# Third contraction chunk of the expert layer as concurrent pairs of 64-row matmuls

## The chip, the cores and the metric

The kernel runs on one core of a Trainium2 chip. The metric is the device time of one execution in microseconds. Before the change it is 226.39 us, the median of three runs (226.37 to 228.31). The profiled execution has a span of 228.9 us, at a mean granted TensorE clock of 0.948.

## What is computed

A gated recurrence (an mLSTM cell) over 4 batches x 8 heads x 768 steps with head dimension 40 gives 3,072 tokens of 320 values. Each token then goes through one of eight experts, the one with the largest router logit:

```python
logits = x @ w_gate                              # [3072, 320] @ [320, 8]
expert_idx = np.argmax(logits, axis=1)
gate_w = softmax(logits)[np.arange(N), expert_idx]
for e in range(E):                               # rows of expert e
    h = np.maximum(x_sorted[lo:hi] @ w1[e], 0.0) # w1[e]: [320, 1024]
    y_sorted[lo:hi] = h @ w2[e]                  # w2[e]: [1024, 320]
y = gate_w[:, None] * y_sorted[inv_perm]
```

The change concerns `x_sorted @ w1[e]`. Its contraction is over 320 = 128 + 128 + 64, three chunks.

## The kernel before, in words

The first half (line 580, `for s in range(-3, NT)`) goes through the recurrence in 24 blocks of 128 tokens, all heads at once: scores, causal mask, attention-like products, a carried state, then router logits and the slot of every token in a DRAM buffer sorted by expert. All of it is recorded in an order written out by hand (`tc.manual_schedule()`, line 279): each engine takes its instructions in the order of the program text.

The second half is the expert layers. Work is cut into groups of `n` blocks of 128 tokens of one expert. Each expert has a first group with n = 2 (256 tokens) and a second with n = 1; six extra groups with n = 1 (`XU`) take what is over, their expert is known only at run time, and their weights are copied from the resident ones by `fetch` (line 758). A loop over further extras (line 812) is entered only if more are needed. The first groups of experts 0 and 1 ("early groups") are written into the end of the first half, in memory and PSUM buffers that the first half no longer needs; their output rows `zo` lie in the old `v1` buffers. The other groups follow in `order` (line 774), in the loop of line 788.

One group goes through these steps:

- `targets` or `aim`, then `turn` (line 226): TensorE transposes the tokens' rows, n x 3 transposes of 128 columns into one PSUM tile `tp`; VectorE copies it to `xT`. The third transpose takes columns 192 to 319 (`wch`), so that its upper 64 rows hold the third chunk and its lower 64 rows repeat columns of the second.
- `layer1` (line 236), in units `u` of 4/n feature blocks of 128: a unit is one PSUM bank `hp` of 512 columns. For every feature block three matmuls of 128 rows accumulate the chunks. The relu out of PSUM into `h` is VectorE's for even units and ScalarE's for odd ones. There are four units for n = 2, two for n = 1.
- `layer2` (line 255) per 128 tokens: eight matmuls of 320 columns accumulate in `zp`, in the order of the feature blocks; ScalarE copies to `zo`, and GpSimd starts a DMA that scatters the rows to `out`.

The transposes of the next group stand between layer 1 and layer 2 of the present one (`ready(groups[i + 1])`, line 799). Since TensorE's order is the program's, a wait at layer 2 holds the next group's layer 1.

The weights of all experts stay in SBUF as bf16: `w1_all` (line 160) has three chunks of 1,024 columns for each expert, in chunk three only rows 64 to 127 with data. Rows 0 to 63 of it are set to zero by VectorE (line 594, once in each of the iterations s = 0 to 7), so that a matmul over 128 rows adds nothing from them. `weights_in` and `weights_out` (lines 173 and 183) load one expert by three DMAs from GpSimd's software queue, converting from float32. They are called at points in the program text for expert after expert; the scatters of tokens and output rows share this queue. PSUM in the second half: three `hp` banks, three `zp`, two `tp` (line 733).

Of the kernel before, what the change touches and what calls it, by code (L numbers as in the profile page):

```python
# [8 lines left out]
F32 = mybir.dt.float32  # L9
BF16 = mybir.dt.bfloat16  # L10
# [5 lines left out]
PSUM = bass.MemoryType.PSUM  # L16
# [3 lines left out]
def kernel(  # L20
# [24 lines left out]
    DP = 64  # L45
# [11 lines left out]

    wch = [d0 if dsz == 128 else Dm - 128 for d0, dsz in dch]
    assert NT * 128 == N and FB * 128 == F and D <= DP
# [100 lines left out]
    w1_all = big.tile([128, DB, E, F], BF16)  # L160
# [12 lines left out]
    def weights_in(e0, n, dbs=((0, 2), (2, 3))):  # L173
        e = slice(e0, e0 + n)
        for a, b in dbs:
            d0, d1 = dch[a][0], sum(dch[b - 1])
            r = min(128, d1 - d0)
            nc.gpsimd.dma_start(
                w1_all[128 - r :, a:b, e, :].rearrange("p a e f -> p (a e) f"),
                moe_w1[e, d0:d1, :].rearrange("e (a p) f -> p (a e) f", p=r),  # L180
            )
# [44 lines left out]
    def turn(g):  # L226
        n = g["n"]
        src = g["xg"] if "xg" in g else xg[g["e"]][g["k"]]
        g["xT"] = spot("xT", [128, DB, n * 128], BF16)
        tp = spot("tp", [128, DB, n * 128], BF16)  # L230
        for j in range(n):
            for db in range(DB):
                nc.tensor.transpose(tp[:, db, j * 128 : (j + 1) * 128], src[:, j, wch[db] : wch[db] + 128], ident_b[:])
        nc.vector.tensor_copy(g["xT"], tp)

    def layer1(g, u):
        n = g["n"]
        per = 4 // n
        if u == 0:
            g["h"] = spot("h", [128, FB, n * 128], BF16)  # L240
        hp = spot("hp", [128, per, n * 128], F32)
        for i in range(per):
            fb = u * per + i
            for db in range(DB):
                nc.tensor.matmul(  # L245
                    hp[:, i, :], lhsT=g["w"][0][:, db, fb * 128 : (fb + 1) * 128], rhs=g["xT"][:, db, :],
                    start=(i == 0 and db == 0), stop=(db == DB - 1), skip_group_check=True,
                )
        dst = g["h"][:, u * per : (u + 1) * per, :]
        if u % 2 == 0:  # L250
            nc.vector.tensor_relu(dst, hp)  # L251
        else:
            nc.scalar.activation(dst, hp, AF.Relu)  # L253

    def layer2(g, j):
        zp = spot("zp", [128, Dm], F32)
# [23 lines left out]
    with tc.tile_pool(name="ring", bufs=1) as ring_pool, \  # L280
# [299 lines left out]
        for s in range(-3, NT):  # L580
# [12 lines left out]
            if 0 <= s < E:  # L593
                nc.vector.memset(w1_all[:64, DB - 1, s, :], 0.0)
# [48 lines left out]
        early = [dict(e=e, n=NE, k=0, si=0) for e in range(2)]  # L643
        spots.update(
            hp=[("sA", ps1), ("sB", ps1)], zp=[("tk", ps1), ("tq", ps1)], tp=[("dC", ps1)],
# [4 lines left out]
        for g in early:  # L650
            g["w"] = (w1_all[:, :, g["e"], :], w2_all[:, g["e"]])
# [43 lines left out]
    def extras():  # L695
# [37 lines left out]
        k: ctx.enter_context(tc.tile_pool(name="moe_" + k, bufs=n, space=PSUM)) for k, n in (("hp", 3), ("zp", 3), ("tp", 2))  # L733
# [24 lines left out]
    def fetch(ex):  # L758
        wx1 = wk_pool.tile([128, DB, F], BF16, name="wx1", bufs=XW)
        wx2 = wk_pool.tile([128, FB, Dm], BF16, name="wx2", bufs=XW)  # L760
        nc.sync.dma_start(wx1[:], w1_all[:, :, bass.ds(ex, 1), :].rearrange("p a e b -> p a (e b)"))
        nc.sync.dma_start(wx2[:].rearrange("p a b -> p (a b)"), w2_all[:, bass.ds(ex, 1)].rearrange("p e a b -> p (e a b)"))
        return wx1, wx2
# [8 lines left out]
    for e in range(E):  # L772
# [3 lines left out]
        dict(e=e, n=(NE, NJ - NE)[k], k=k, si=(0, NE)[k], w=(w1_all[:, :, e, :], w2_all[:, e])) for e, k in order  # L776
# [75 lines left out]
```

## Time and profile before

| | |
|---|---|
| time, median of 3 | 226.39 us |
| span of the profiled execution | 228.9 us |
| TensorE busy (matmuls) | 198.4 us, 87% |
| TensorE weight loads, beside matmuls | 167.9 us, 73% |
| VectorE / ScalarE / GpSimd busy | 56% / 52% / 56% |
| moved by DMA | 46.5 MB, mean 203 GB/s |
| layer 1 matmuls (line 245) in the stretch after 160 us | 312 of 128 columns, 96 of 256 columns |

A line of the timeline has the start in us, the time in us (from the start of the first to the end of the last of equal instructions in a row), the engine, the line in the kernel, the operation, `out<-in`, the shapes and the number of instructions; in brackets the idle time of the engine before it, and what ended it. "PE" is TensorE's matmuls, "PEld" its weight loads, "DVE" VectorE, "ACT" ScalarE, "POOL" GpSimd. Matmuls are pipelined, so the start of one to the start of the next is much less than the time of one; the ends are modelled. In the page's slices each digit is the busy share of 1/40 of the span in tenths, 9 being 90% or more.

### The profile page before, as it was taken

What the parts mean: (1) busy time and instruction counts of PE and PEld (TensorE: products, weight loads), DVE (VectorE), ACT (ScalarE), POOL (GpSimd) and SP (SyncE); (2) the same over time, 40 slices, a digit from 0 to 9 for tenths busy, and PEclk for the clock granted to TensorE, in tenths of its full rate; (3) what the DMA queues carried; (4) which work ended last, traced back from release to release, by engine and by line L of the source; (5) the groups of instructions that cost most, each with busy time, mean ns of one, the idle gap of its engine ahead of it and who ended that gap; (6) DMA issues with size and microseconds to landing.
All of it is one profiled execution on the core that took longest, in us unless ns stands there. A gap on an engine that the chain in (4) does not pass through costs nothing.

```text
span 228.9 us, 5771 instructions
## 1 busy us (share of the span) xinstructions
PE 198.4 (87%) x2054; PEld 167.9 (73%) x2063; DVE 128.4 (56%) x421; ACT 118.2 (52%) x275; POOL 129.2 (56%) x219
## 2 busy tenths in 40 slices
PE   2299999999999998899999968983999798989990
PEld 2168788889989998688788756862887586867760
DVE  7648778797678785877635423315454152333330
ACT  3458758789688887859321632430243333333330
POOL 5046696465678887679687298365455333333331
PEclk9999999999999999999855999997699999999996
DMA  7999999999999989999999999999999969966900
GB/s 138 178 190 190 188 203 168 203 207 207 171 164 188 167 161 175 201 162 169 163 314 194 190 149 176 252 224 218 220 265 212 239 247 369 386 231 248 366 28 4
DMA packets 122158, 46.50 MB, mean 203 GB/s; under 512 B 102474, under 2 KB 114893, under 8 KB 122128
## 3 DMA queue, kind: packets, MB, share of 16 engines
q1 hardware_dynamic: 107424, 27.52, 56.4%
q0 software_dynamic: 14240, 18.38, 38.7%
q8 instruction: 17, 0.28, 0.5%
q10 hardware_dynamic: 464, 0.21, 0.4%
q14 instruction: 13, 0.11, 0.2%
HBM read 39.38 MB, written 9.53 MB: 214 GB/s over the span
## 4 chain that ended last, share of the span: by engine, by line
PE 35%; DMA 26%; issue 16%; POOL 9%; DVE 8%; ACT 3%; POOLq 1%; SPq 0%; ACTq 0%
DMA w_all<-in_moe_w_dram 15%; POOL out_dram L265 8%; PE hp L447 7%; PE hp L379 6%; DMA out_dram<-zo,s_idx 6%; PE dC L387 4%; DMA v<-in_v_dram 4%; PE tk L341 3%; PE xt L424 3%; PE tq L341 3%; PE sA L354 2%; PE sA L359 2%; DMA kq<-in_q_dram 2%; PE hp L399 2%; DVE kq L88 1%
## 5 line engine op out<-in xcount | busy, mean ns | idle before, releaser
L265 POOL DMA_INDIRECT out_dram<-zo,s_idx x20 | 20.0, 998 | 31.2 <-ACT zo L263 22.7
L245 PEld LDWEIGHTS <-w_all 128*128 128x128 bf16 x384 | 31.4, 102 | 6.8 <-issue 2.5
L251 DVE TENSOR_SCALAR h<-hp 128x512 bf16<-128x512 f32 x26 | 18.0, 691 | 32.7 <-PE hp L245 30.8
L258 PE MATMUL zp<-w_all,h 128*128 128x320 bf16 x160 | 26.1, 310 | 8.2 <-DVE s_idx L207 4.9
L258 PEld LDWEIGHTS <-h 128*128 128x128 bf16 x208 | 18.4, 100 | 19.4 <-DVE h L251 6.9
L253 ACT ACTIVATE h<-hp 128x512 bf16<-128x512 f32 x26 | 15.5, 597 | 30.2 <-PE hp L245 20.3
L552 POOL DMA_INDIRECT x_sorted<-x_all,slots x24 | 25.0, 1043 | 10.6 <-ACT x_all L546 6.5
L245 PE MATMUL hp<-xT,w_all 128*128 128x128 bf16 (+1 forms) x336 | 30.0, 249 | 0.8 <-DMA w_all<-in_moe_w_dram 0.8
L417 POOL TENSOR_TENSOR x_sb<-x_sb,den 128x320 f32<-128x320 f32 x23 | 16.7, 725 | 21.0 <-DVE den L415 19.8
L263 ACT COPY zo<-zp 128x320 f32<-128x320 f32 x26 | 11.1, 425 | 25.6 <-PE zp L258 25.0
L379 PE MATMUL hp<-C_sb,qT 104*128 104x82 f32 x160 | 22.4, 286 | 0.5 <-DVE lgs L457 0.5
L379 PEld LDWEIGHTS hp<-C_sb,qT 104*128 104x128 f32 x160 | 21.1, 205 | 0.7 <-DVE lgs L457 0.6
L426 ACT COPY xT<-xt 128x384 f32<-128x384 f32 x24 | 11.6, 483 | 18.2 <-PE xt L424 13.3
L366 ACT CAST dB<-sB 128x512 bf16<-128x512 f32 x24 | 14.0, 582 | 12.6 <-PE sB L360 9.6
L341 PE MATMUL tk<-ident,kq 128*104 128x128 f32 x96 | 16.4, 296 | 4.0 <-DMA kq<-in_k_dram 4.0
L447 PE MATMUL hp<-wg_sb,xT 128*128 128x8 f32 x144 | 19.0, 264 | 0.0
L387 PE MATMUL dC<-vA,kq 128*104 128x82 f32 x160 | 18.6, 261 | 0.0
L447 PEld LDWEIGHTS hp<-wg_sb,xT 128*128 128x128 f32 x144 | 18.2, 203 | 0.0
L329 POOL CAST vAb<-vA 128x328 bf16<-128x328 f32 x24 | 11.0, 460 | 11.9 <-DVE vA L327 11.9
L367 POOL TENSOR_SCALAR_AFFINE_SELECT dB<-dB 128x512 bf16<-128x512 bf16 x24 | 16.3, 680 | 1.9 <-ACT dB L366 1.7
L327 DVE TENSOR_TENSOR vA<-v,G_T 128x328 f32<-128x328 f32 x24 | 15.3, 639 | 3.3 <-DMA v<-in_v_dram 3.2
L364 DVE TENSOR_TENSOR dA<-sA,cmask 128x512 bf16<-128x512 f32 x24 | 16.0, 665 | 1.9 <-PE sA L359 1.9
(150 smaller groups left out, 441.3 us busy)
## 6 DMA issues: line engine op xcount, KB each, us to landing
w_all<-in_moe_w_dram POOLq DMA_DIRECT2D x8, 640.0 KB
wx<-w_all SPq DMA_DIRECT2D x6, 768.0 KB
w_all<-in_moe_w_dram POOLq DMA_DIRECT2D x8, 512.0 KB
kq<-in_k_dram SPq DMA_DIRECT2D x24, 160.0 KB
kq<-in_q_dram SPq DMA_DIRECT2D x24, 160.0 KB
v<-in_v_dram SPq DMA_DIRECT2D x24, 160.0 KB
o_sb<-in_o_gate_dram SPq DMA_DIRECT2D x24, 160.0 KB
wx<-w_all SPq DMA_DIRECT2D x6, 640.0 KB
```

Of the source, the lines that this page charges most:

```text
L245: nc.tensor.matmul(hp[:, i, :], lhsT=g["w"][0][:, db, fb * 128 : (fb + 1) * 128], rhs=g["xT"][:, db, :], start=(i == 0 and db == 0), stop= ...
L251: nc.vector.tensor_relu(dst, hp)
L258: nc.tensor.matmul(zp, lhsT=g["h"][:, fb, j * 128 : (j + 1) * 128], rhs=g["w"][1][:, fb, :], start=(fb == 0), stop=(fb == FB - 1),)
L265: ins = nc.gpsimd.indirect_dma_start(out=out[:, :], out_offset=bass.IndirectOffsetOnAxis(ap=at, axis=0), in_=zo, in_offset=None, bounds_ch ...
L341: nc.tensor.transpose(tp[:, j, :], two(d[n], j), ident[:])
L364: nc.vector.tensor_tensor(d["dA"][:], sA[:], cmask[:, None, :].to_broadcast([128, PR, 128]), op=ALU.mult)
L367: nc.gpsimd.affine_select(d["dB"][:], d["dB"][:], compare_op=ALU.is_ge, fill=0.0, base=0, pattern=[[0, PR], [1, 128]], channel_multiplier=-1,)
L379: nc.tensor.matmul(hp[:, 2 * j * D1 : (2 * j + 2) * D1], lhsT=d["qT"][:, j, :], rhs=st["C"][:, j].rearrange("p h d -> p (h d)"), start=(j ...
L387: nc.tensor.matmul(st["dC"][:, j], lhsT=two(d["k"], j), rhs=d["vA"][:, 2 * j : 2 * j + 2, :], start=(c == 0 and j == 0), stop=True, skip_g ...
L417: eng.tensor_tensor(x3d, x3d, den[:].unsqueeze(2).to_broadcast([128, H, D]), op=ALU.mult)
L447: nc.tensor.matmul(lg[:, i * E : (i + 1) * E], lhsT=st[t]["xT"][:, db * 128 : (db + 1) * 128], rhs=wg_sb[:, db, :], start=(fresh and i == ...
L552: ins = nc.gpsimd.indirect_dma_start(out=xs[:, :], out_offset=bass.IndirectOffsetOnAxis(ap=slots[:, t : t + 1], axis=0), in_=x_all[:, t, : ...
```

## The change

The third chunk fills only half of the array's rows. The change runs it as pairs of matmuls over 64 rows each: the third chunk's weights of feature blocks 0 to 3 lie in partitions 0 to 63 and those of blocks 4 to 7 in partitions 64 to 127 ("folded"), and one matmul of each half runs in the lower and the upper 64 rows of the array at once, into two PSUM banks. The aim is to spend the time of half as many matmuls on the third chunk, and to drop the zeros.

What follows from it:

- the tokens' third chunk must lie in both halves of the partitions, so its transpose is made twice, each of 64 columns, into rows 0 to 63 and rows 64 to 127 of `tp`;
- units go in twos: at an even unit two `hp` banks are taken and the pairs for both written first; then the unit's two full chunks follow, and the odd unit's after it. Even units are feature blocks 0 to 3 (VectorE's relu), odd ones 4 to 7 (ScalarE's);
- `w1_all` has 2,560 columns for each expert instead of 3,072; the third chunk is loaded by two DMAs (one for each half) in place of one; the zeroing on VectorE is gone;
- PSUM has four `hp` and two `zp` banks. In the early groups `hp` goes through four banks (`sA`, `sB`, `tk`, `tq`), which `zp` shares.

```diff
-    w1_all = big.tile([128, DB, E, F], BF16)
+    w1_all = big.tile([128, E, FL * F + F // 2], BF16)
...
-    def weights_in(e0, n, dbs=((0, 2), (2, 3))):
-        e = slice(e0, e0 + n)
-        for a, b in dbs:
-            d0, d1 = dch[a][0], sum(dch[b - 1])
-            r = min(128, d1 - d0)
+    def weights_in(e, n=1):
+        nc.gpsimd.dma_start(
+            w1_all[:, e, : FL * F].rearrange("p (a f) -> p a f", f=F),
+            moe_w1[e, : FL * 128, :].rearrange("(a p) f -> p a f", p=128),
+        )
+        for i in range(2):
             nc.gpsimd.dma_start(
-                w1_all[128 - r :, a:b, e, :].rearrange("p a e f -> p (a e) f"),
-                moe_w1[e, d0:d1, :].rearrange("e (a p) f -> p (a e) f", p=r),
+                w1_all[64 * i : 64 * i + 64, e, FL * F :], moe_w1[e, FL * 128 :, i * HF * 128 : (i + 1) * HF * 128],
             )
...
-                nc.tensor.transpose(tp[:, db, j * 128 : (j + 1) * 128], src[:, j, wch[db] : wch[db] + 128], ident_b[:])
+                at = src[:, j, db * 128 : min(Dm, (db + 1) * 128)]
+                if db < FL:
+                    nc.tensor.transpose(tp[:, db, j * 128 : (j + 1) * 128], at, ident_b[:])
+                    continue
+                for r in range(2):
+                    nc.tensor.transpose(tp[64 * r : 64 * r + 64, db, j * 128 : (j + 1) * 128], at, ident_b[:])
...
-        hp = spot("hp", [128, per, n * 128], F32)
+        if u % 2 == 0:
+            g["hp"] = [spot("hp", [128, per, n * 128], F32) for _ in range(2)]
+            for i in range(per):
+                for a in range(2):
+                    c = FL * F + (v + i) * 128
+                    r = slice(64 * a, 64 * a + 64)
+                    nc.tensor.matmul(
+                        g["hp"][a][:, i, :], lhsT=w[r, c : c + 128], rhs=xT[r, FL, :], start=(i == 0), stop=False,
+                        skip_group_check=True,
+                    )
+        a = u % 2
+        hp = g["hp"][a]
         for i in range(per):
-            fb = u * per + i
-            for db in range(DB):
+            for db in range(FL):
+                c = db * F + (a * HF + v + i) * 128
                 nc.tensor.matmul(
-                    hp[:, i, :], lhsT=g["w"][0][:, db, fb * 128 : (fb + 1) * 128], rhs=g["xT"][:, db, :],
-                    start=(i == 0 and db == 0), stop=(db == DB - 1), skip_group_check=True,
+                    hp[:, i, :], lhsT=w[:, c : c + 128], rhs=xT[:, db, :], start=False, stop=(db == FL - 1),
+                    skip_group_check=True,
                 )
-        dst = g["h"][:, u * per : (u + 1) * per, :]
-        if u % 2 == 0:
+        dst = g["h"][:, a * HF + v : a * HF + v + per, :]
+        if a == 0:
             nc.vector.tensor_relu(dst, hp)
...
-        zp = spot("zp", [128, Dm], F32)
+        zp = spot(g.get("zp", "zp"), [128, Dm], F32)
...
-            if 0 <= s < E:
-                nc.vector.memset(w1_all[:64, DB - 1, s, :], 0.0)
...
-        early = [dict(e=e, n=NE, k=0, si=0) for e in range(2)]
+        early = [dict(e=e, n=NE, k=0, si=0, zp="hp") for e in range(2)]
         spots.update(
-            hp=[("sA", ps1), ("sB", ps1)], zp=[("tk", ps1), ("tq", ps1)], tp=[("dC", ps1)],
+            hp=[(t_, ps1) for t_ in ("sA", "sB", "tk", "tq")], tp=[("dC", ps1)],
...
-("hp", 3), ("zp", 3), ("tp", 2)
+("hp", 4), ("zp", 2), ("tp", 2)
...
-        wx1 = wk_pool.tile([128, DB, F], BF16, name="wx1", bufs=XW)
+        wx1 = wk_pool.tile([128, FL * F + F // 2], BF16, name="wx1", bufs=XW)
```

Here `FL` is the index of the third chunk (2), `HF` half the number of feature blocks (4), and `F` is 1,024.

## The prediction

> **What bounds the kernel now.** I read the page's 40 slices first, then the busy time by stretch, then the timeline around the stops of TensorE and of single groups of tokens, and last the attention half for an operation like the new one. The page's rows for TensorE and the DMA engines:
>
> ```profile
> PE   2299999999999998899999968983999798989990
> DMA  7999999999999989999999999999999969966900
> ```
>
> A slice is 5.7 us. The DMA engines are full for the first 32 slices; TensorE has a hole in slices 27 and 28 (154 to 160 us) and is nearly full after it. So there are two regimes, and the timeline has the line where one hands over to the other:
>
> ```profile
> 156.44 0.33 DVE L697 TENSOR_TENSOR og<-tot,thr 128x168 f32<-128x168 f32 x1 [6.38 <-DMA out_dram<-v,s_idx]
> 158.20 2.31 PE L258 MATMUL zp<-w_all,h 128*128 128x320 bf16 x8 [4.86 <-DVE s_idx L207]
> ```
>
> VectorE's `og` takes over memory of the attention half and waits until the last output rows of the two early groups have left it. Those rows stand in the software DMA queue behind the weights of expert 4. TensorE stops for 4.86 us for this. Before 158.2 us the queue sets the time, and a quicker layer 1 only lengthens the stop. After 158.2 TensorE works in program order to the end (223.5): four groups of 256 tokens ("n=2") and thirteen of 128 ("n=1": seven second parts and six extras). Only these can be made faster or slower.
>
> An n=2 group is bound by TensorE alone (columns: start, us, engine, line):
>
> ```profile
> 185.10 2.78 PE L245 MATMUL hp<-xT,w_all 128*128 128x256 bf16 x24
> 187.72 0.33 PE L233 MATMUL tp<-ident_b,x_all 128*128 128x128 bf16 x3
> 187.88 2.34 PE L258 MATMUL zp<-w_all,h 128*128 128x320 bf16 x16
> ```
>
> Layer 1 is 24 x 0.109 = 2.62 us, then three transposes at 0.056, then 16 x 0.136 of layer 2, without a gap. (Spacing is total less the modelled 0.27 us end, over 23.) An n=1 group is not:
>
> ```profile
> 205.66 1.50 PE L245 MATMUL hp<-xT,wx 128*128 128x128 bf16 x24
> 206.59 0.69 DVE L251 TENSOR_SCALAR h<-hp 128x512 bf16<-128x512 f32 x1 [1.16 <-PE hp L245]
> 207.00 0.33 PE L233 MATMUL tp<-ident_b,xgx 128*128 128x128 bf16 x3
> 207.25 0.60 ACT L253 ACTIVATE h<-hp 128x512 bf16<-128x512 f32 x1 [0.96 <-PE hp L245]
> 207.34 1.28 PE L258 MATMUL zp<-wx,h 128*128 128x320 bf16 x8
> 208.46 1.50 PE L245 MATMUL hp<-xT,wx 128*128 128x128 bf16 x24
> ```
>
> Work on TensorE is 24 x 0.056 + 3 x 0.056 + 8 x 0.136 = 2.60 us, but the period is 2.80: layer 2 cannot start before VectorE's relu of the first half (206.59 + 0.69 = 207.28, seen at 207.34). What starts that relu is the twelfth matmul, 0.615 us into layer 1. Its time in the group is what counts, not how long layer 1 is.
>
> **What the Trainium skill says.** "TensorE: Matmul & The Clock Gate", Part 3, The mechanism: matmuls in different row groups run side by side, starts some 4 ns apart. "TensorEngine Tiling (Array Packing)", Key Properties: "Changing tiling mode (not just tile) drains the TensorE", with no figure. The attention half has both, since lines 359 and 360 are matmuls of 40 rows in the lower and the upper 64 rows of the array:
>
> ```profile
> 49.93 0.38 PE L354 MATMUL sA<-dA,ident_b 128*128 128x512 bf16 x1
> 50.24 0.23 PE L359 MATMUL sA<-qb,kb 40*128 40x128 bf16 x1
> 50.24 0.23 PE L360 MATMUL sB<-qb,kb 40*128 40x128 bf16 x1
> 50.31 0.22 PE L359 MATMUL sA<-qb,kb 40*128 40x128 bf16 x1
> 50.42 0.22 PE L359 MATMUL sA<-qb,kb 40*128 40x128 bf16 x1
> 50.42 0.22 PE L360 MATMUL sB<-qb,kb 40*128 40x128 bf16 x1
> 50.57 0.42 PE L341 MATMUL tk<-ident,kq 128*104 128x128 f32 x2
> ```
>
> The trace agrees with both pages. A pair starts together, and the next pair about 0.056 us later: a pair costs one matmul. Going in, the 512-column matmul of 49.93 is followed after 0.31 us, where three of them in the chain take 0.65 (0.217 each): 0.09 us more. Going out, 50.42 to 50.57 is 0.15 where 0.056 would do: 0.09 again. So one block of pairs costs two changes, 0.18 us, and about 0.02 more as the second matmul after a change comes some 0.01 late: 0.20 us.
>
> **The change part by part.** *Pairs in layer 1, n=2.* Per two units four third-chunk matmuls become two pairs: saved 2 x 0.109 = 0.22; added one block, 0.20 less 0.02 for whole-array successors that hide part. Two blocks a group: 2 x (0.22 - 0.20) = -0.04 us.
>
> *Pairs in layer 1, n=1.* Eight matmuls become four pairs, 0.22 saved, one block, 0.20 paid: TensorE's own time is unchanged. The order matters more. The pairs of both halves now come first. The first half is then finished after four pairs and eight matmuls, 12 x 0.056, exactly as many slots as before, plus both changes: VectorE's relu starts 0.20 later and layer 2 with it, about 1.87 instead of 1.67 us into the group. The second half is 0.04 earlier, which nothing needs. The old period was held at 2.80 by the ScalarE half (0.03 later than VectorE's), so the loss is 1.87 + 1.10 - 2.80, about +0.18 us.
>
> *Transposes.* The third chunk (64 columns) is transposed twice, into PSUM rows 0-63 and 64-127: one matmul more for each 128 tokens, in another tiling mode (64-column tiles). The trace of before has no such tile. Low bound: the two run side by side and the mode costs nothing, 0. High bound: two changes as for row tiles and no overlap, 0.18 + 0.06 = 0.24. I take 0.19, two changes and overlap, as the skill's sentence speaks of any change of mode. It lies on the path where TensorE is the bound: behind n=2 groups, -0.04 + 0.19 = +0.15. In an n=1 group followed by n=1, layer 1 ends at 1.32 and the transposes at 1.69, under the relu's 1.87: hidden. Followed by n=2 there are two token blocks: 1.32 + 0.73 = 2.05, past 1.87, so the loss is 2.05 + 1.10 - 2.80 = +0.35.
>
> *Weight loads.* Per expert one DMA of 64 rows x 2,048 bytes becomes two of 64 x 1,024. The packet records of the queue have 188 ns for 2,048 bytes and 71 for 640; between them 1,024 bytes is about 105 (estimate). 128 x 105 - 64 x 188 = 1.4 us of engine time, 0.09 on 16 engines; five experts stand ahead of the handover: +0.4 us. Each DMA also takes GpSimd about 0.68 us to issue, and since a DMA waits for the one eight places before it on its semaphore, GpSimd stops more often: the output rows of the early groups queue behind it, the last issued near 148 instead of 144. They stand behind expert 4's weights anyway, which keep the queue full past 154, so that costs nothing.
>
> *With one answer.* Eight memsets (8 x 0.485 us of VectorE before 49 us) go: the loads fill the DMA engines there, nothing gained. Four `hp` buffers and two `zp`: two `zp` suffice, since each is copied out in 0.43 us and reused 1.1 us later at the earliest. Copying 640 KB for 768 KB per extra: loaded ahead, hidden. The early groups' new PSUM buffers lie before the handover.
>
> *Sum.* Of the nine n=1 groups followed by n=1 or the end, three (179.5, 200.7, 210.1 us) had layer 2's second half held by a late signal from TensorE to ScalarE, which would hide a later start: 6 x 0.18 = 1.1. Of the four followed by n=2, one (192.0) likewise: 3 x 0.35 = 1.05. n=2: 4 x 0.15 = 0.6. Weights 0.4. Total +3.15 us: 226.39 + 3.1 = 229.5.
>
> **The rivals.** *Column tiles cost no change of mode.* Then the n=1 to n=2 case falls to 0.18 (0.55 in all), n=2 to -0.04 (-0.15): 1.1 + 0.55 - 0.15 + 0.4 = +1.9, 228.3. For it: no column tile is in the trace; against it: the skill's wording. *Changes of mode vanish between bf16 matmuls.* Then n=1 is level (12 slots before, 12 after), n=2 gains 4 x 0.44 = 1.75, the weights still cost 0.4: -1.35, 225.0, faster. For it: the way out was seen only towards an fp32 transpose, whose slow weight load may be the 0.09; against it: the way in is bf16 to bf16 and shows 0.09, also behind line 399 (0.114 against 0.024). *Pairs do not overlap* with these operands: 13 x 0.22 + 4 x 0.44 = 4.6 more, 234.1. Against it: the pairs of lines 359 and 360 do, into two PSUM banks, as here.
>
> **How the numbers follow.** Forecast 0.58, rival one 0.20, rival two 0.15, rival three 0.07. The late signals, which cost up to 1.3 us each and come at no fixed place, add about 1 us either way. Range 226.2 to 231.5: it leaves out rival two and rival three. Faster 0.15; same 0.22 (most of rival one and the low edge of the forecast); slower 0.63.
>
> **What would show it.** In the profile after: pairs starting together, 0.2 us of changes about each block; in the extras' stage a period near 2.97 instead of 2.80, with VectorE's relu starting some 1.04 us after the first pair (0.93 after the first matmul before); behind n=2 groups transposes of about 0.36 us; the handover at 158.2 to 158.8. The prediction is wrong if the extras' period stays at 2.80 or falls, if a block of pairs takes under 0.3 us with its changes for n=1, or if the handover moves by over a microsecond.

## The result, and the profile after

The changed kernel takes 234.28 us (median of 4, 233.21 to 235.63) where the kernel before, beside it, takes 227.35: a ratio of 1.032, 95% interval 1.022 to 1.042. It is slower, and by more than the 231.5 us at which the range ended.

The kernel before itself differs between the sets of runs below (220.8 to 228.7 us), so every number is a ratio to the runs of the kernel before in its own set, and timelines are compared only at one level: 221 or 228 us.

The rows of the page for TensorE and the DMA engines after the change keep the two regimes, with the hole of TensorE in slices 27 and 28 again (151 to 162 us):

```profile
PE   2299999999999999998998979907899899899980
DMA  8999999998999999927799999999999799717600
```

The timeline around the handover (columns here and below: start, us, engine, line, operation, shapes, idle before):

```profile
156.38 0.33 DVE L715 TENSOR_TENSOR og<-tot,thr 128x168 f32<-128x168 f32 x1 [9.75 <-DMA w_all<-in_moe_w_dram]
158.15 2.32 PE L278 MATMUL zp<-w_all,h 128*128 128x320 bf16 x8 [8.02 <-DVE s_idx L209]
```

`og` starts where it did in the profile of before (156.44), but TensorE now stops for 8.02 us where it stopped for 4.86. That profile of before was of an execution of 230.69 us, above its median of 227.35, while this one (233.57) is near its own. So the equal start does not show an unmoved handover; the experiments must. An n=2 group, and the transposes behind it:

```profile
195.07 0.39 PE L256 MATMUL hp<-xT,w_all 64*128 64x256 bf16 x4
195.40 1.05 PE L265 MATMUL hp<-xT,w_all 128*128 128x256 bf16 x8
196.38 0.39 PE L256 MATMUL hp<-xT,w_all 64*128 64x256 bf16 x4
197.58 0.28 PE L237 MATMUL tp<-ident_b,x_all 128*128 128x128 bf16 x2
197.79 0.25 PE L240 MATMUL tp<-ident_b,x_all 128*64 128x128 bf16 x2
197.97 2.35 PE L278 MATMUL zp<-w_all,h 128*128 128x320 bf16 x16
200.25 0.40 PE L256 MATMUL hp<-xT,w_all 64*128 64x128 bf16 x8
```

The pairs overlap: two pairs of 256 columns and the change out of their mode take 195.40 - 195.07 = 0.33 us, which is 2 x 0.109 + 0.11. The eight full matmuls and the change into the mode take 196.38 - 195.40 = 0.98, which is 8 x 0.109 + 0.11. A block thus costs 0.22 us of changes, and saves the 0.22 of two matmuls. The transposes take 197.97 - 197.58 = 0.39 us where they took 0.16: 0.23 more for 128 tokens. The group's period is 5.18 us; it was 4.96. And one of the extras:

```profile
213.48 0.40 PE L256 MATMUL hp<-xT,wx 64*128 64x128 bf16 x8
213.81 1.07 PE L265 MATMUL hp<-xT,wx 128*128 128x128 bf16 x16
214.52 0.69 DVE L271 TENSOR_SCALAR h<-hp 128x512 bf16<-128x512 f32 x1 [1.27 <-PE hp L265]
214.71 0.28 PE L237 MATMUL tp<-ident_b,xgx 128*128 128x128 bf16 x2
214.91 0.25 PE L240 MATMUL tp<-ident_b,xgx 128*64 128x128 bf16 x2
215.27 1.27 PE L278 MATMUL zp<-wx,h 128*128 128x320 bf16 x8
216.47 0.40 PE L256 MATMUL hp<-xT,wx 64*128 64x128 bf16 x8
```

VectorE's relu starts 1.04 us after the first pair, layer 2 follows its end (215.21) at 215.27, and the period is 2.99 against 2.80. Everything in the second regime looks nearly as forecast. So which part made the loss twice as large?

### The profile page after: what moved, and what is told of

Same layout as the page of the kernel before. It is cut to its first block, busy times and chain, and to the rows that moved or that the text cites. A ratio compares the mean times of both kernels' runs of the same rounds, so it can differ in the third digit from the quotient of the medians.

```text
span 231.8 us, 5829 instructions
## 1 busy us (share of the span) xinstructions
PE 197.8 (85%) x2084; PEld 155.6 (67%) x2093; DVE 124.6 (54%) x413; ACT 118.1 (51%) x275; POOL 133.4 (58%) x227
## 4 chain that ended last, share of the span: by engine, by line
PE 46%; issue 17%; POOL 16%; DVE 10%; ACT 5%; DMA 4%; POOLq 1%; ACTq 0%; DVEq 0%
POOL out_dram L285 8%; PE hp L265 5%; PE hp L467 5%; PE hp L399 4%; PE tk L361 4%; PE zp L278 4%; PE dC L407 4%; DMA w_all<-in_moe_w_dram 4%; PE tq L361 3%; PE xt L444 3%; PE sA L374 3%; PE sA L379 3%; POOL x_sb L437 2%; PE hp L256 2%; POOL x_sorted L572 2%
## 5 line engine op out<-in xcount | busy, mean ns | idle before, releaser
L265 PEld LDWEIGHTS <-w_all 128*128 128x128 bf16 x256 | 18.4, 98 | 5.4 <-issue 3.4
L265 PE MATMUL hp<-xT,w_all 128*128 128x128 bf16 (+1 forms) x224 | 21.2, 244 | 0.0
L361 PE MATMUL tk<-ident,kq 128*104 128x128 f32 x96 | 17.2, 307 | 4.2 <-DMA kq<-in_k_dram 4.2
L399 PE MATMUL hp<-C_sb,qT 104*128 104x82 f32 x160 | 20.6, 272 | 0.0
L399 PEld LDWEIGHTS hp<-C_sb,qT 104*128 104x128 f32 x160 | 19.4, 192 | 0.3
L467 PE MATMUL hp<-wg_sb,xT 128*128 128x8 f32 x144 | 17.7, 255 | 0.0
L407 PEld LDWEIGHTS dC<-vA,kq 128*104 128x104 f32 x160 | 17.1, 178 | 0.0
L467 PEld LDWEIGHTS hp<-wg_sb,xT 128*128 128x128 f32 x144 | 17.0, 192 | 0.0
```

Of the source, the lines that this page charges most:

```text
L265: nc.tensor.matmul(hp[:, i, :], lhsT=w[:, c : c + 128], rhs=xT[:, db, :], start=False, stop=(db == FL - 1), skip_group_check=True,)
L361: nc.tensor.transpose(tp[:, j, :], two(d[n], j), ident[:])
L399: nc.tensor.matmul(hp[:, 2 * j * D1 : (2 * j + 2) * D1], lhsT=d["qT"][:, j, :], rhs=st["C"][:, j].rearrange("p h d -> p (h d)"), start=(j ...
L407: nc.tensor.matmul(st["dC"][:, j], lhsT=two(d["k"], j), rhs=d["vA"][:, 2 * j : 2 * j + 2, :], start=(c == 0 and j == 0), stop=True, skip_g ...
L467: nc.tensor.matmul(lg[:, i * E : (i + 1) * E], lhsT=st[t]["xT"][:, db * 128 : (db + 1) * 128], rhs=wg_sb[:, db, :], start=(fresh and i == ...
```

## The experiments

### One part at a time

Theory A was that all of the loss lies in the groups behind the handover, as the two profiles have it (some 3 us). Theory B was that 7 us are real, and that something outside those groups, such as the first half, costs some 3 us more. Four kernels in one set, the kernel before at 221.25 us. First the changed kernel again:

> The changed kernel itself, timed in turns with the kernel before on one chip. The profile of the changed kernel is 2.9 us longer than that of the kernel before (231.8 against 228.9), the timed medians differ by 6.9 us (234.28 against 227.35). Theory A (all of the change is in the groups after the handover at 158 us, as the profile shows): ratio 1.012 to 1.016, some +3 us. Theory B (something outside the profiled difference, such as the DMA-bound first half, costs 3 us more in unprofiled runs): ratio 1.025 to 1.035, +6 to +8 us.

Measured: 228.1 us, 1.0318 (1.0255 to 1.0381), +6.9 us. Theory A falls on its size. Theory B is left, but where its 3 us lie is not shown by this run. Then the pairs and the loads with the old transposes:

```diff
-                at = src[:, j, db * 128 : min(Dm, (db + 1) * 128)]
-                if db < FL:
-                    nc.tensor.transpose(tp[:, db, j * 128 : (j + 1) * 128], at, ident_b[:])
-                    continue
-                for r in range(2):
-                    nc.tensor.transpose(tp[64 * r : 64 * r + 64, db, j * 128 : (j + 1) * 128], at, ident_b[:])
+                nc.tensor.transpose(tp[:, db, j * 128 : (j + 1) * 128], src[:, j, wch[db] : wch[db] + 128], ident_b[:])
```

Here the lower halves of the pairs multiply columns 192 to 255 in place of 256 to 319; the amount of work is that of the pairs.

> The changed kernel with the old three transposes of 128 columns for each 128 tokens in place of the two in 64-column tiles. Leaves out: rows 0 to 63 of the third chunk hold the tokens' columns 192 to 255 instead of 256 to 319, so half of the feature blocks multiply other values; the amount of work is that of the change. Theory A (64-column tiles cost two changes of tiling mode): transposes for an n=1 group take 0.17 us instead of 0.39, n=2 groups 5.18 to 4.96, n=1 groups before an n=2 group 3.2 to 2.97, n=1 before n=1 unchanged at 2.99; about 1.7 us less than the changed kernel, +1.2 us against the kernel before. Rival (column tiles cost nothing of note): as the changed kernel within 0.5 us.

Measured: 227.3 us, 1.0266 (1.0202 to 1.0330). The timeline of one of its extras has the relu wait bare:

```profile
207.46 0.40 PE L251 MATMUL hp<-xT,wx 64*128 64x128 bf16 x8
208.51 0.69 DVE L266 TENSOR_SCALAR h<-hp 128x512 bf16<-128x512 f32 x1 [1.96 <-ACT zo L278]
209.26 1.26 PE L273 MATMUL zp<-wx,h 128*128 128x320 bf16 x8 [0.23 <-DVE h L266]
210.45 0.40 PE L251 MATMUL hp<-xT,wx 64*128 64x128 bf16 x8
```

TensorE is through with its transposes and idles 0.23 us for VectorE's relu. The period is 2.99 whatever group follows. Next the double transposes alone, on the kernel before:

```diff
-                nc.tensor.transpose(tp[:, db, j * 128 : (j + 1) * 128], src[:, j, wch[db] : wch[db] + 128], ident_b[:])
+                if db < DB - 1:
+                    nc.tensor.transpose(tp[:, db, j * 128 : (j + 1) * 128], src[:, j, wch[db] : wch[db] + 128], ident_b[:])
+                    continue
+                for r in range(2):
+                    nc.tensor.transpose(
+                        tp[64 * r : 64 * r + 64, db, j * 128 : (j + 1) * 128], src[:, j, db * 128 : Dm], ident_b[:]
+                    )
```

> The kernel before with the third chunk transposed twice in 64-column tiles (rows 0 to 63 meet the zeros in the weights), nothing else changed. Theory A: +0.22 us for each 128 tokens where TensorE is the bound, behind n=2 groups and between n=1 and n=2: 4 x 0.2 + 4 x 0.35 = +2.2 us at most, +0.8 at least as n=1 groups have up to 0.2 us of idle TensorE; the n=1 to n=1 period stays at 2.80. Rival (column tiles free): within 0.3 us of the kernel before.

Measured: 224.41 us, 1.0182 (1.0123 to 1.0241): 4.0 us, where the expectation had 2.2 at most. The timeline has both kinds of group:

```profile
189.16 0.28 PE L234 MATMUL tp<-ident_b,x_all 128*128 128x128 bf16 x2
189.36 0.25 PE L237 MATMUL tp<-ident_b,x_all 128*64 128x128 bf16 x2
189.54 2.35 PE L264 MATMUL zp<-w_all,h 128*128 128x320 bf16 x16
191.73 1.50 PE L251 MATMUL hp<-xT,w_all 128*128 128x128 bf16 x24
193.07 0.28 PE L234 MATMUL tp<-ident_b,x_all 128*128 128x128 bf16 x2
193.45 1.26 PE L264 MATMUL zp<-w_all,h 128*128 128x320 bf16 x8
194.55 1.50 PE L251 MATMUL hp<-xT,w_all 128*128 128x128 bf16 x24
```

The transposes take 0.38 us in both. Behind n=2 the period rises by 0.23 (5.19). From n=1 to n=1 it is 194.55 - 191.73 = 2.82, where the relu was waited for anyway. From n=1 to n=2 it is 3.22 against 2.80. Last the loads alone, the third chunk of the kernel before by two DMAs of half its columns (64 rows of 1,024 bytes). Here and in some code excerpts below only the lines that come in are shown:

```diff
+        nc.gpsimd.dma_start(
+            w1_all[:, : DB - 1, e, :], moe_w1[e, : (DB - 1) * 128, :].rearrange("(a p) f -> p a f", p=128),
+        )
+        for i in range(2):
+            c = slice(i * (F // 2), (i + 1) * (F // 2))
+            nc.gpsimd.dma_start(w1_all[64:, DB - 1, e, c], moe_w1[e, (DB - 1) * 128 :, c])
```

> The kernel before with the third chunk's weights loaded by two DMAs of 64 rows x 1,024 bytes in place of one of 64 x 2,048 bytes, nothing else changed. Theory A (the queue only gets 0.09 us of work more for each expert): the end of TensorE's stop moves from 158.2 by at most 0.5 us, time +0 to +0.5 us. Theory B (GpSimd's stops on DMAs eight places back, or the shorter rows, hold the queue): handover and time later by 2 us or more.

Measured: 223.33 us, 1.0108 (1.0047 to 1.0169), 2.4 us of 221.25. All periods of the second regime are those of before (4.96 and 2.80). So the cost came ahead of it, and the traces show where. There is no trace of the kernel before at this level. A kernel of a later set stands in for it, the one with an unused tile of 2,080 bytes: it has the loads, the TensorE program and the time (0.9983) of the kernel before. Its last two DMAs of output rows of the early groups, `og`, and the first layer of expert 4, then the same four of the loads alone:

```profile
139.08 1.04 POOL L267 DMA_INDIRECT out_dram<-v,s_idx  x1 [0.30 <-ACT zo L265]
140.43 1.02 POOL L267 DMA_INDIRECT out_dram<-v,s_idx  x1 [0.30 <-issue]
150.99 0.33 DVE L699 TENSOR_TENSOR og<-tot,thr 128x168 f32<-128x168 f32 x1 [9.18 <-DMA out_dram<-v,s_idx]
158.79 2.78 PE L247 MATMUL hp<-xT,w_all 128*128 128x256 bf16 x24
```

```profile
141.43 1.04 POOL L263 DMA_INDIRECT out_dram<-v,s_idx  x1 [0.30 <-issue]
145.34 1.02 POOL L263 DMA_INDIRECT out_dram<-v,s_idx  x1 [2.87 <-issue]
154.54 0.33 DVE L695 TENSOR_TENSOR og<-tot,thr 128x168 f32<-128x168 f32 x1 [11.38 <-DMA w_all<-in_moe_w_dram]
161.91 2.78 PE L243 MATMUL hp<-xT,w_all 128*128 128x256 bf16 x24
```

GpSimd issues the last rows 4.9 us later, and `og` starts 3.6 and expert 4's group 3.1 us later. The time at which the last rows are issued parts the traces at this level by their loads (those slowed by a moved tile, below, left out): with the loads of before it is 140.4 to 141.6 us, with the added DMA 144.5 to 147.2. (At 228 us: 142.4 to 144.2, and 146.8 to 148.6; only the changed kernel with loads for two, below, has its last rows at 146.7 with no more loads than before, behind a stop of 3.30 us for ScalarE.) A single `og` is a weaker sign: one kernel with the loads of before, in an execution of 223.47 us where its median is 222.05, has it at 154.21.

The parts do not add: 1.8 for the transposes, 1.1 for the loads and 2.66 - 1.08 = 1.6 per cent for the pairs make 4.5, and together they cost 3.2. The periods say a part of why:

| period, us | n=2 | n=1 to n=2 | n=1 to n=1 |
|---|---|---|---|
| kernel before, loads alone | 4.96 | 2.80 | 2.80 |
| transposes alone | 5.19 | 3.22 | 2.82 |
| pairs and loads | 5.03 | 2.99 | 2.99 |
| changed kernel | 5.18 | 3.21 | 2.99 |

In an n=1 group layer 2 waits for two chains, the transposes on TensorE and the relu on VectorE. The longer one counts, so each edit hides behind the other. By the table this is worth 4 x 0.08 + 3 x 0.20 + 9 x 0.02 = 1.1 us (the groups are counted in the next paragraph), of a gap of 1.3 per cent or 2.9 us. Most of what is left lies in the transposes alone: their periods make 4 x 0.23 + 3 x 0.42 + 9 x 0.02 = 2.4 us, where 4.0 (2.7 to 5.3) were measured. Where the other 1.6 are was not found; their trace is of the fastest of seven executions, 222.21 us.

Whether the second regime explains the rest is read from the start of the group of expert 4 (n = 2) to the end of the span. With the loads alone (above) it starts at 161.91 of 221.8 us, in the changed kernel of the same set at 162.17 of 226.2:

```profile
162.17 0.39 PE L256 MATMUL hp<-xT,w_all 64*128 64x256 bf16 x4
```

That is 59.9 us and 64.0: +4.1. By the table, with four n=2 groups, three n=1 groups ahead of an n=2 and nine other n=1 groups, 4 x 0.22 + 3 x 0.41 + 9 x 0.19 = 3.8; one group, the last ahead of the extras, took 3.34 instead of 2.99. Its relu started 1.40 us after the first pair instead of 1.04, also with the old transposes; why was not found. With the loads the sum is 4.1 + 2.4 = 6.5 of the 6.9 measured.

### What is it in the loads?

Two things differ between one load of the third chunk and two: one DMA more for each expert, and rows of half the length. Four kernels in a second set, the kernel before at 228.74 us. A DMA more without shorter rows:

```diff
+        for r0, r1 in ((0, 63), (63, 64)):
+            nc.gpsimd.dma_start(
+                w1_all[64 + r0 : 64 + r1, DB - 1, e, :], moe_w1[e, (DB - 1) * 128 + r0 : (DB - 1) * 128 + r1, :],
+            )
```

> The kernel before, with the load of each expert's third chunk cut by rows instead of columns: 63 rows and 1 row of 2,048 bytes, so one DMA more for each expert and no shorter rows (not a byte more is moved). Theory of the count (each extra DMA makes GpSimd stop on the semaphore of an earlier one, so that what is queued behind it is issued later): og starts near 154.5 us as with the two half-width loads, not near 151 as with one load, and the time is 1.5 to 2.5 us over the kernel before. Theory of the short rows (1,024-byte rows move worse): og as with one load, time within 0.4 us of the kernel before.

Measured: 231.51 us, 1.0136 (1.0092 to 1.0180). Then shorter rows without a DMA more:

```diff
-    w1_all = big.tile([128, DB, E, F], BF16)
+    w1_all = big.tile([128, DB, E, F + 64], BF16)
...
+        t = w1_all[64:, DB - 1, e, :].rearrange("p (h f) -> p h f", h=2)[:, :, : F // 2]
+        nc.gpsimd.dma_start(t, moe_w1[e, (DB - 1) * 128 :, :].rearrange("p (h f) -> p h f", h=2))
```

> The kernel before, with the third chunk still loaded by one DMA for each expert but in 128 rows of 1,024 bytes (a gap of 32 columns between the halves of its place in SBUF; the gaps are zeroed). Theory of the count: within 0.5 us of the kernel before, og near 151. Theory of the short rows: og near 154.5, time 1.5 to 2.5 us over the kernel before.

Measured: 229.63 us, 1.0002 (0.9968 to 1.0036). Its wider `w1_all` also moves all later tiles, by 3,072 bytes. So in these two kernels shorter rows cost nothing, and a DMA of a single row more for each expert costs 3.1 us. Next the changed kernel with fewer loads:

```diff
-        for i in range(2):
+        for i in range(2 if e % 2 == 0 else 0):
             nc.gpsimd.dma_start(
-                w1_all[64 * i : 64 * i + 64, e, FL * F :], moe_w1[e, FL * 128 :, i * HF * 128 : (i + 1) * HF * 128],
+                w1_all[64 * i : 64 * i + 64, e : e + 2, FL * F :],
+                moe_w1[e : e + 2, FL * 128 :, i * HF * 128 : (i + 1) * HF * 128].rearrange("e p f -> p e f"),
```

> The changed kernel, with the two half-width loads of the third chunk issued for two experts at once at every second expert, so that the count is three for two experts' pair of chunks, back to that of the kernel before on average, with the same short rows. Theory of the count: og near 151 and the time 1.5 to 2.3 us under the changed kernel, so 4.5 to 5.5 us over the kernel before (ratio 1.020 to 1.025). Theory of the short rows: as the changed kernel, ratio 1.031. A third outcome: the bytes of the odd expert loaded earlier than they are needed push back what the handover waits for, and og comes later still.

Measured: 233.05 us, 1.0193 (1.0141 to 1.0246), against 1.032 with all the loads: 2.9 us back, about what the loads had cost; the 1.032 are of other sets. (The fourth kernel of this set is told below, under the relu wait.)

GpSimd is what an added DMA can hold up: 0.5 to 0.8 us to issue it, and its wait for an earlier DMA. (In the traces its DMAs take eight semaphores in turn, and a DMA waits for its own semaphore, that is for the DMA eight places before it.) The view of what GpSimd waited for between 104 and 158 us has, of waits for DMAs, for the kernel before and then for the fourth load (columns: waiting output and line, releaser, us in all, times, longest):

```profile
POOL w_all L178 <- DMA w_all<-in_moe_w_dram: 4.2, 2, 3.1
POOL out_dram L265 <- DMA w_all<-in_moe_w_dram: 0.5, 1, 0.5
```

```profile
POOL w_all L184 <- DMA w_all<-in_moe_w_dram: 4.6, 3, 3.4
POOL w_all L178 <- DMA w_all<-in_moe_w_dram: 3.8, 2, 2.2
```

4.7 us of waits for weight loads become 8.4. Counted alike in every trace, they are 7.8 to 9.9 us in the six kernels with the added DMA, and at most 6.0 in the twelve without it; the changed kernel with loads for two has 1.4. So these waits go with the added DMA. They are not shown to be the whole cause: in the two kernels of before with an added DMA, the stop just ahead of the last output rows (2.87 us in the lines above, 2.19 with the fourth load) has no releaser in the profile. What remains is to take the issuing time away from the DMA: a memset of 0.6 us in its place.

> The kernel before, with a memset of 128 x 560 bf16 on GpSimd (0.6 us, an unused tile) behind each expert's first-layer loads: it takes as much of GpSimd as issuing a fourth DMA would, without a DMA and its semaphore. Theory of the stops (a DMA more makes GpSimd wait for the one eight places before it): ratio 1.000 to 1.003. Rival, the issuing time on GpSimd itself delays what stands behind: 1.010 to 1.015, as with the fourth load.

Measured (third set, kernel before 227.93): 238.37 us, 1.0421 (1.0358 to 1.0485). Neither theory allows this. In its profile, of an execution of 246.07 us, expert 2's first layer starts at 157.38 us where it starts at 141.59 in the kernel before, and the kernel had got a new tile of 1,120 bytes behind `w2_all`, which moved the place of every later tile. So the same memset went to rows that hold zeros already:

```diff
+        nc.gpsimd.memset(w1_all[:64, DB - 1, e0, :560], 0.0)
```

> The kernel before, with a memset of 64 x 560 bf16 on GpSimd (about 0.6 us) behind each expert's first-layer loads, into the part of w1_all that VectorE had zeroed already, so that no tile is added and no address moves. Theory of the stops: ratio 1.000 to 1.003, and the 1.042 of the memset into a tile of its own came from that tile's place in memory. Theory of the issuing time: 1.010 to 1.015. If it is 1.042 again, the memset itself holds up the attention half.

Measured (fourth set, kernel before 221.2): 222.05 us, 1.0009 (0.9981 to 1.0036). GpSimd's time for issuing, as far as a memset stands for it, costs nothing. And the tile without the memsets:

```diff
+    pad = big.tile([128, 560], BF16)
+    nc.gpsimd.memset(pad[:, :8], 0.0)
```

> The kernel before, with only the unused tile of 1,120 bytes for each partition behind w2_all (one memset of eight columns at the start): every tile after it moves by 1,120 bytes, which is 32 bytes off a multiple of 64. Theory of the place: ratio near 1.04, with loads of the attention half that take longer. Theory that the memsets of 0.6 us cost it: 0.998 to 1.002.

Measured: 230.32 us, 1.0301 (1.0234 to 1.0367). The place alone costs 3.0 of the 4.2 per cent; the intervals just overlap, and what the rest is was not tested. To see whether alignment does it, the same tile with 1,152 bytes (a multiple of 64) and with 2,080 (not one):

> The kernel before with an unused tile of 1,152 bytes for each partition behind w2_all, a multiple of 64. Theory of the alignment: ratio 0.997 to 1.003, rows of 160 bytes in the attention half at 15 ns in the mean. Theory that any moved address costs it: near 1.03, rows at 19 ns.

> The same with 2,080 bytes, 2,048 and 32. Theory of the alignment: near 1.03, rows of 160 bytes at 19 ns in the mean, as with 1,120. Theory that the one address of 1,120 was unlucky: 0.997 to 1.003.

Measured (fifth set, kernel before 220.81): 231.44 us, 1.0311 (1.0233 to 1.0388) with 1,152; 220.67 us, 0.9983 (0.9957 to 1.0008) with 2,080. It is the reverse of what the alignment theory expected; it falls. In the packet records the 98,304 rows of 160 bytes that load the attention half take 18.9 to 19.1 ns in the mean with 1,120 and 1,152 bytes and 14.8 to 15.2 in every other kernel here, with a median of 14 in all: a tenth of the rows take 29 ns or more there, where elsewhere nine tenths take 14 or less. The three profiles with 19 ns are of executions longer than their kernels' medians; two other such profiles, with short rows and with the memset in place, have 15.0. The queue's row of the page, for 1,152 bytes (an execution of 237.38 us) and for 2,080 (220.18; packets, MB, share of 16 engines):

```profile
q1 hardware_dynamic: 107424, 27.52, 64.8%
```

```profile
q1 hardware_dynamic: 107424, 27.52, 58.0%
```

For the case, what counts is that the changed kernel, which moves later tiles by 8,192 bytes, has 14.9 ns: its loss does not come from there.

Then the count was taken the other way, on the kernel before: the third chunk loaded for two experts at a time, half a DMA less for each.

```diff
+        for e0, n, a, b in ((e, 1, 0, 2), (e, 2, 2, 3)):
+            if a == 2 and e % 2:
+                break
```

> The kernel before, with the third chunk loaded by one DMA for two experts at every second expert: half a DMA less for each expert, rows as before. Theory of the count in the other direction: GpSimd stops less, og comes 1 to 1.5 us earlier, ratio 0.992 to 0.996. Rival (only an added stop hurts; with the count of before the queue is full anyway): 0.998 to 1.002. Against both: the weights of the odd expert come before those that are needed next, which could cost up to 1 us.

Measured (third set): 228.18 us, 1.0020 (0.9991 to 1.0048). Half a DMA less gains nothing. Either the loss begins only beyond the count of before, or the gain is used up by the odd expert's weights, which now come earlier than they are needed; no run separates the two. Shown is: a DMA more for each expert costs 1.1 per cent as two half loads and 1.4 as 63 rows and one, and with it the last output rows are issued later; short rows and GpSimd's time for issuing do not cost it. That the loss comes from GpSimd's waits for earlier DMAs is in part argued: they go with the added DMA in all traces, but no run changed them alone. Two rivals stay untested: a fixed time that each DMA takes in the queue itself and, for the fourth load alone, a worse share of 63 rows and one among 16 DMA engines.

### The relu wait

If VectorE's relu sets an n=1 group's period, TensorE should get work that does not wait for it: the next group's layer 1 ahead of this group's layer 2.

```diff
+    ready(groups[0])
+    first_layer(0)
+    ready(groups[1])
     for i, g in enumerate(groups):
...
-        for u in range(FB * g["n"] // 4):
-            layer1(g, u)
-        if i + 1 < len(groups):
-            ready(groups[i + 1])
+        first_layer(i + 1)
+        if i + 2 < len(groups):
+            ready(groups[i + 2])
```

> The kernel before, with the first layer of the next group issued on TensorE ahead of the second layer of the present one, so that no relu is waited for. If the 0.2 us by which an n=1 group's period (2.80) exceeds its work on TensorE (2.60) is the wait for the relu, the extras' period falls to 2.60 to 2.65 and 13 groups give 2.0 to 2.6 us: ratio 0.988 to 0.991. If something else sets the period (the output rows that GpSimd issues, PSUM buffers coming free), it stays near 2.80 and the time within 0.5 us.

Measured (second set): 223.52 us, 0.9787 (0.9733 to 0.9841), faster than the kernel before, and by more than the 0.988 to 0.991 expected. Its timeline at the end, one period of 2.59 us without a stop:

```profile
209.62 1.50 PE L245 MATMUL hp<-xT,wx 128*128 128x128 bf16 x24
210.96 0.33 PE L233 MATMUL tp<-ident_b,xgx 128*128 128x128 bf16 x3
211.13 1.25 PE L258 MATMUL zp<-wx,h 128*128 128x320 bf16 x8
212.21 1.50 PE L245 MATMUL hp<-xT,wx 128*128 128x128 bf16 x24
```

(Some extras still take 2.7 to 2.8.) The same order on the changed kernel:

> The changed kernel (three loads of first-layer weights for each expert, pairs, 64-column transposes) with the first layer of the next group issued ahead of the second layer of the present one, so that no relu is waited for. Theory: what the pairs alone cost in an n=1 group was the later relu of the first half, and that is hidden now; what stays is TensorE's own time: pairs level (20 x 0.056 + 0.20 against 24 x 0.056), transposes 0.39 for 0.17, so the extras' period is 2.80 against 2.60 of the kernel before in that order. With the loads: 13 x 0.2 + 4 x 0.2 + 2.1 = 5.5 us more than the kernel before in that order, so a ratio of 1.001 to 1.005 to the kernel before. Rival, the blocks of pairs cost TensorE itself more than they save: a period of 2.9 or more, ratio 1.010 or more.

Measured (third set): 227.54 us, 0.9991 (0.9962 to 1.0020), against 1.001 to 1.005 expected. The period is what the theory says it would be:

```profile
210.04 0.40 PE L256 MATMUL hp<-xT,wx 64*128 64x128 bf16 x8
210.37 1.07 PE L265 MATMUL hp<-xT,wx 128*128 128x128 bf16 x16
211.27 0.28 PE L237 MATMUL tp<-ident_b,xgx 128*128 128x128 bf16 x2
211.66 1.26 PE L278 MATMUL zp<-wx,h 128*128 128x320 bf16 x8
```

Layer 1 with its changes is 211.27 - 210.04 = 1.23 from its first pair; the change into the pairs, about 0.1, lies before it. So it takes 1.33 where it took 24 x 0.056 = 1.34: level. The transposes are 0.39 for 0.17, and the next pair comes at 212.85, 2.81 us on. With nothing waiting for a relu, the pairs cost TensorE nothing, and the transposes 0.22. Last, this order with the loads for two experts at a time:

> The kernel before with both edits: third chunk loaded for two experts at a time, and the first layer of the next group ahead of the second of the present one. If the two gains lie in different stages (up to og, and after it) they add: the ratio of the order alone (0.979) less what the loads for two give alone, so 0.972 to 0.980.

Measured: 222.17 us, 0.9760 (0.9714 to 0.9807), the fastest here. Its interval overlaps that of the order alone. Why did the order bring 2.1 per cent, twice what the relu waits make? The two kernels with loads for two, in the old order and then in the new one, show it at the handover:

```profile
154.69 0.33 DVE L699 TENSOR_TENSOR og<-tot,thr 128x168 f32<-128x168 f32 x1 [7.58 <-DMA out_dram<-v,s_idx]
156.45 2.31 PE L260 MATMUL zp<-w_all,h 128*128 128x320 bf16 x8 [6.05 <-DVE s_idx L209]
162.69 2.78 PE L247 MATMUL hp<-xT,w_all 128*128 128x256 bf16 x24
```

```profile
152.13 1.25 PE L260 MATMUL zp<-w_all,h 128*128 128x320 bf16 x8
154.85 0.33 DVE L699 TENSOR_TENSOR og<-tot,thr 128x168 f32<-128x168 f32 x1 [6.00 <-DMA out_dram<-v,s_idx]
157.15 4.37 PE L247 MATMUL hp<-xT,w_all 128*128 128x256 bf16 x24 [3.77 <-DVE xT L236]
```

`og` starts at nearly the same time. In the old order the layer 2 that waited for it is followed by a whole n=1 group before expert 4's layer 1 starts at 162.69. In the new order that layer 2 stands at 152.13, ahead of the stop, and expert 4's layer 1 starts at 157.15. It has one layer 2 of 1.1 us still owing, so TensorE is 162.69 - 157.15 - 1.1 = 4.4 us further on. From there to the ends (226.1 and 219.5) the new order gains 2.1 more, close to the least that was expected. This is a net sum: in it the old order has three further stops of about 1.0 us each; the new has two, of 1.16 and 0.39, and expert 4's first layer takes 4.37 us in place of 2.78. The relu wait itself is seen more cleanly in the extras' 2.59 for 2.80. The expectation had only this second part.

## Why the prediction was wrong, point by point

- **The two regimes** were right: the loads alone change no period after the handover, and the transposes and pairs change those as computed.
- **A block of pairs, 0.20 us** for 0.22 saved: right (0.22). "TensorEngine Tiling (Array Packing)", Key Properties, was rightly taken for both kinds of change; it gives no figure, and the trace has about 0.10 to 0.11 us for each. For n=2 groups the forecast had a gain of 0.04 us all the same; with the old transposes they lose 0.07 (5.03 for 4.96), so the saving there was nothing.
- **The relu of the first half 0.20 later, period 2.97**: right; 1.04 us after the first pair as written, 2.99. The runs with the old transposes (a bare wait of 0.23 us) and with layer 1 ahead (no loss from pairs) show the cause.
- **Transposes, 0.19 for 128 tokens**: slightly small, 0.22 to 0.23, near the upper bound of 0.24. From n=1 to n=2 the loss is 0.41, not 0.35; behind n=2 it is 0.22 in all, not 0.15.
- **Late signals that hide some of it**: right for the set in which it was predicted, where the n=1 groups of experts 2 to 7 take 3.21, 3.93, 3.21, 3.93, 3.91 and 3.34 us in the changed kernel and 2.80, 4.25, 2.92, 3.99, 3.91 and 2.80 in the kernel with the fourth load, at the same level with TensorE's program as before: the three that are held longest are not longer for the change. In the timelines of the sets at 221 us no such signals appear, and nothing is hidden. In both the ratio of the changed kernel is 1.032, so this doesn't explain the miss. (The longest held group of before takes 4.38 us, 1.6 over 2.80; the forecast had up to 1.3 for one signal.)
- **Weight loads, +0.4 us**: this step failed. The forecast put the cost down to shorter rows. It foresaw that GpSimd would issue the early groups' last output rows later ("near 148 instead of 144"; 146.8 in the changed kernel, 148.6 with the fourth load, 144.1 before) and put that at nothing, as they stand behind expert 4's weights "anyway, which keep the queue full past 154". The measured cost is 2.4 us (loads alone) and 3.1 (fourth load), and the rows' share is nothing. A full queue does not protect: with the loads alone the rows are issued 4.9 us later, and `og` follows 3.6 later. The handover moved by 3.1 us there, more than the one microsecond that was to show the prediction wrong. This is the largest missing term, 2 to 2.7 us of some 3.8.
- **The sum.** 3.15 predicted; 6.9 measured at both levels. At 221 us: loads 2.4 in place of 0.4; TensorE 4.1 from expert 4's first group on, where the forecast's own terms without hidden ones give 9 x 0.18 + 3 x 0.35 + 4 x 0.15 = 3.3. The rest of that 0.8 is the larger transposes and the one group of 3.34 (0.35). And 0.4 us is unassigned, well inside the interval. At 228 us expert 4's group and all behind it take 67.9 us in the changed kernel and 64.7 with the fourth load: 3.2, and 3.1 for the added DMA.
- **The rivals.** Column tiles without a change of mode, changes that vanish between bf16 matmuls, pairs that don't overlap: the timeline after rules out all three. The third rival's number, 234.1, is the measured one by chance: its 4.6 us for pairs that do not overlap are not there, and stand where the loads and larger transposes do. None of them was about the loads; the range was built on TensorE alone, with the loads as a constant.

## What to carry to other kernels

Where a software queue sets a stage, count its DMAs, not only its bytes: here a single-row DMA more for each expert cost as much as a load cut in two, while half a DMA less gained nothing. A transfer that is issued later can matter though the queue ahead of it is full: look at who waits for its landing. Packing two half-height matmuls into one slot is worth only what it saves less two changes of tiling mode (here 0.22 less 0.22), and everything that must be rearranged for it comes on top; look also at which partial result becomes ready later. And where TensorE waits for a relu in its own program order, put independent work into that place first: a change of order alone brought 2 per cent here, and the timelines put more than half of it at another stop than the one it was meant for.

## What the runs showed that was not expected

An unused tile of 1,120 or of 1,152 bytes for each partition, which only moves the tiles behind it, made the kernel before 3.0 and 3.1 per cent slower; one of 2,080 bytes didn't (0.9983). The rows of 160 bytes then take 19 ns in the mean instead of 15, at the same median of 14. Alignment to 64 bytes is not the cause, and what is stays open. A memset of 0.6 us into such a tile had looked like a cost of 4.2 per cent; put where no tile moves, it cost none.
